# Memory attention and token/channel mixer on one core: an attention schedule with shifted due times

## The chip, the cores and the metric

The kernel runs on one core of a Trainium2 chip. The metric is device time in microseconds (us) of one execution, from the launch to the end. The core's engines are TensorE (PE in the profile, with PEld for its weight loads), VectorE (DVE), ScalarE (ACT), GpSimd (POOL) and SyncE (SP, which issues DMAs only). Each engine takes its instructions in the order in which the program recorded them, and waits for the others by semaphores.

## The reference

Eight batches of eight heads, 576 tokens, head size 64, 32 memory slots. The attention first pools keys and values into the slots and then lets the queries attend to them. A mixer follows: over tokens (576 to 256 to 576) and over channels (512 to 1536 to 512), both with a residual.

```python
a = softmax(phi, axis=2)                    # over the tokens' 32 memory scores
k_m = einsum('bhsm,bhsd->bhmd', a, k)
v_m = einsum('bhsm,bhsd->bhmd', a, v)
attn = softmax(q @ k_m.T / sqrt(64), axis=-1)
x = attn @ v_m                              # to (batch, 576, 512)
h = relu(x.T @ w_tok1) @ w_tok2
u = x + h.T
out = u + relu(u @ w_ch1) @ w_ch2
```

## The kernel before

**The products.** Full float32 precision is had from float32r matmuls: each operand is kept as a high part (a rounded copy, made by ScalarE) and a low part (the rest, a subtraction by VectorE, or by GpSimd at a few places), and each product is three matmuls: high by high, high by low, low by high. Nearly all operands therefore pass through ScalarE, then VectorE, before TensorE can use them.

**The work.** The channel mixer runs over nine chunks of 512 tokens. Chunks 0 to 2 are done plainly (line 161 the first product `cp`, 126 and 129 the parts `hh` and `hl` of its relu, 184 the second product into `acc`). From chunk 3 on the first product is built from seven smaller products of quarters, in the tiles `qa` and `qb` (line 322); ScalarE copies them to `whole` (1917), VectorE adds there (1920), and lines 126 and 129 split the relu into `qhh` (or `qal`'s high tile) and `qhl` (or `qal`). The second product (184) of the pair before is mixed in between.

**The attention beside it.** A quad `(b, Q)` is four heads of batch `b`. Its work is one long chain through all engines. `phi` is loaded (line 407), reduced over tokens by VectorE (421, `pr`) and across partitions by GpSimd (432, `prr`), subtracted (435), raised (ACT, 445), and summed (421 and 454). `step_kv` (467) pools keys and values. `scales`, `turn_keys`, `spread_v` (458 to 516) scale them; the keys go through memory and back (519, 528) to become `kb`. `step_s` (566) makes the scores `sp` in two PSUM banks, VectorE turns them (573), and the softmax follows (580 to 597). VectorE turns the result into `aT` (603); `a_pair` makes its high part on ScalarE (638) and its low part (639) on `low_eng`: GpSimd, but VectorE in quads (2,0) and (4,0). `v_pair` (652) then writes `vv` on ScalarE, in the room of `aT`, so it has to wait for the low parts. The softmax also goes to memory as `rows` (663) and comes back as `raw` (670, 673); `nat_full` and `nat_tail` split it (122, 123); `step_A` (708) and `step_R` (727) are the token mixer's first product, each split again (`Ah`, `Al`; `Rh`, `Rl`); `step_u` (748), four times, gives the chunk's input `u`.

**What sets the order.** Attention and mixer share each engine's queue by a table of due times. A unit is one product of the mixer (a chunk has 24), a step is entered with `at(h, fn, k=...)`, and the loop over the mixer calls what is due at its point of the program, in the order of `h`, then `k` (-1, 0, 1), then entry. In chunks 1 and 2, what is due at an even `h` with `k=0` stands ahead of the twelve matmuls of the second product there, and with `k=1` behind them. For each quad, `m` is the unit of `step_kv` and `r` an offset for the scores; `JOINT = (4, 1)` marks the last quad that has its `step_kv` alone. From (5,0) on `step_kv` rides along with the `step_s` of the quad before. `w` shifts the steps of `phi`. The table of quads is `starts` (line 1779): (3,0) has m=38, r=44; (3,1) 49, 54; (4,0) 59, 63.5; (4,1) 69, 74; then (5,0) 79, 86; (5,1) 91, 98; (6,0) 103, 110 and so on in steps of 12.

Chunk 3 begins at unit 72. PSUM has two banks for all attention tiles (tag `at`), so each of them waits for the one before the last to be read. `phi` has two buffers.

Of the kernel before, what the change touches and what calls it, by code (L numbers as in the profile page):

```python
# [28 lines left out]
def kernel(  # L29
# [36 lines left out]
    NF = 2 * w_ch2.shape[0]  # L66
# [1660 lines left out]
    for Q, h0 in ((0, 3), (1, 11)):  # L1727
        qd = quads[1, Q]
        late = 4 if not Q else 0
# [27 lines left out]
    for z in order:  # L1757
        if z.eng == "PE":
# [3 lines left out]
            if gap > 0.3 and z.take:  # L1762

                late = any(y.eng == "SP" and y.ready > z.begin - 0.5 for y in z.after)
# [10 lines left out]
    def at(h, fn, *x, k=0):  # L1775
        events.setdefault((max(h, 0), k), []).append((fn, x))

    JOINT = (4, 1)
    starts = [(2, 0, 24, 24), (2, 1, 34, 34), (3, 0, 38, 44), (3, 1, 49, 54), (4, 0, 59, 63.5), (4, 1, 69, 74)]
    while starts[-1][:2] != (B - 1, 1):  # L1780
        b, Q, m, r = starts[-1]
        starts.append((b + Q, 1 - Q, r + 5, r + NF))
    for b, Q, m, r in starts:
        qd = second if b == 2 and not Q else Quad(b, Q)
        fine = b > 2
        if (b, Q) == (4, 0):
            qd.low_eng = nc.vector
        if qd is not second:
            at(max(m - 11, 2 * NF), qd.load_phi)
            if fine:  # L1790
                w = 1.5 * ((b, Q) == (5, 0))
                at(m - (6 if (b, Q) == (3, 0) else 8.5 - w), qd.phi_max, k=1)
                w -= 1.5 * (JOINT < (b, Q))
                at(m - 4.5 + w, qd.phi_sub)
                at(m - 4 + w, qd.phi_only_exp)
                w += 1.5 * (JOINT < (b, Q))
                at(m - 3.5 + w, qd.phi_sum)
            else:
                at(m - 7, qd.phi_max, k=1)
                at(m - 3, qd.phi_exp, k=1)  # L1800
                at(m - 2, qd.phi_sum, k=1)
            at(loaded + (5 if (b, Q) > (3, 1) else 1), qd.load_kv, k=1)
            at(r - (3 if fine else 4), qd.load_q, k=1)
        joint = JOINT < (b, Q)
        if joint:
            former.follow, loaded = qd, m - 3
        else:
            at(m, qd.step_kv)
            loaded = m
        qd.follow, former = None, qd  # L1810
        at(r + 2, qd.step_s)
        if fine:
            for x, fn in (
                (m + 0.5, qd.scales), (m + 1, qd.turn_keys), (m + 1.5, qd.spread_v),
                (m + 3.5, qd.get_keys), (m + 5, qd.v_high), (m + 6, qd.v_low),
                (r + 2.5, qd.S_max), (r + 3, qd.sub_exp), (r + 4, qd.S_sum), (r + 4.5, qd.S_mul),
                (r + 4.5, qd.rows_out), (r + 5, qd.turn_pairs), (r + 8, qd.nat_full),
                (r + 8.5, qd.nat_tail), (r + 9.5, qd.step_A), (r + 10.5, qd.step_R),
            ):
                at(x, fn)  # L1820
            at(r + 6, qd.rows_in, "qT", 1)
            for x in range(2):
                at(r + 6 + x / 2, qd.a_pair, x)
                at(r + 7 + x / 2, qd.v_pair, x)
            for x in range(4):
                at(r + 12 + x // 2 * 1.5 + x % 2 / 2, qd.step_u, x // 2, x % 2)
            continue
        at(m + 4, qd.values)
        at(m + 1, qd.step_T)
        at(r + 3, qd.sm2)  # L1830
        at(r + (3 if qd is second else 4), qd.a_pair, 1)
        at(r + 6, qd.nat, k=1)
        at(r + 7, qd.v_pairs)
        at(r + 8, qd.step_A)
        at(r + 9, qd.step_R)
        for x in range(4):
            at(r + 10 + x // 2 * (1 if qd is second else 2), qd.step_u, x // 2, x % 2)
    for c in range(2, CHUNKS):
        h = 2 * NF * (c - 1)
        at(h + (9 if c == 2 else 7 if c <= WIN else 1), lambda c=c: mixer(c).take(), k=1)  # L1840
        if c < WIN:
# [3 lines left out]
        late = (  # L1845
            (-6.5, -3, -2.5, -6.5, -3, -2.5, -3.5, -1, -0.5, -1, -0.5, 0, 0.5)
            if c > WIN
            else (-3.5, -3, -2.5, -3.5, -2, -3, -3, -2, -2.5, 0.5, 0.5, 1, 1)
        )
# [217 lines left out]
```

## Time and profile before

| | |
|---|---|
| Median of 3 runs | 769.16 us (767.67 to 769.16) |
| The profiled execution, in all | 765.83 us |
| Its span, first to last instruction | 764.0 us |
| Granted TensorE clock | 1.000 |
| PE busy | 750.1 us (98%) |
| PEld busy | 651.4 us (85%) |
| DVE busy | 466.3 us (61%) |
| ACT busy | 337.9 us (44%) |
| POOL busy | 106.6 us (14%) |
| DMA, mean over the span | 193 GB/s |

In the rows of the trace a time is the start in us from the span's start, then the duration, engine, line, operation, and what it writes and reads; in square brackets stands the idle time of the engine ahead of it and what ended that. The list of waits gives, for an instruction and what it waited for, the sum in us, how often, and the longest. SPq and ACTq are the parts of SyncE and ScalarE that issue DMAs.

### The profile page before, as it was taken

To read this page: it belongs to the slowest core of one execution; us is meant where nothing else is said; L and a number is where in the kernel's file an instruction comes from. 1 tells how busy PE (TensorE), PEld (TensorE's weight loads), DVE (VectorE), ACT (ScalarE), POOL (GpSimd) and SP (SyncE) were. 2 spreads that over 40 slices of the span, in tenths; PEclk is the share of its full clock that TensorE was granted. 3 is DMA by queue.
4 is the path that set the end of the run, shared out by engine and by line. 5 is a ranking of instruction groups with operands and counts; after the bars stand their busy time and mean duration, and the time that the engine had idled before them with its cause. 6 is when DMAs were issued, how large, how long until landed. Compare 5 with 4: busy or idle time off the path is not lost.

```text
span 764.0 us, 13356 instructions
## 1 busy us (share of the span) xinstructions
PE 750.1 (98%) x5159; PEld 651.4 (85%) x5159; DVE 466.3 (61%) x878; ACT 337.9 (44%) x771; POOL 106.6 (14%) x92
## 2 busy tenths in 40 slices
PE   9999999999999999999999999999999999999998
PEld 8777788777878878889888988888989999998997
DVE  4989874786567656665766558564855255335234
ACT  5897553242315333453443535353635343333331
POOL 2144343002112132020101101010101000000000
PEclk9999999999999999999999999999999999999999
DMA  9945630684825454867576849584757367556661
GB/s 366 414 176 171 226 104 1 152 262 141 272 48 176 145 175 124 290 183 249 155 257 202 287 132 280 182 270 147 200 190 207 113 190 232 169 165 221 193 184 65
DMA packets 90447, 147.35 MB, mean 193 GB/s; under 512 B 41488, under 2 KB 60304, under 8 KB 86160
## 3 DMA queue, kind: packets, MB, share of 16 engines
q1 hardware_dynamic: 69216, 79.77, 31.5%
q10 hardware_dynamic: 21168, 66.73, 28.1%
q8 instruction: 41, 0.67, 0.3%
q14 instruction: 22, 0.18, 0.1%
HBM read 121.57 MB, written 24.90 MB: 192 GB/s over the span
## 4 chain that ended last, share of the span: by engine, by line
PE 60%; DMA 6%; DVE 5%; SPq 2%; ACT 1%; issue 1%; POOL 0%; ACTq 0%; DVEq 0%; POOLq 0%
PE acc L184 26%; PE qa L322 12%; PE qb L322 9%; PE u L748 5%; PE cp L161 3%; DMA phi<-in_phi_dram 3%; SPq L519 1%; PE Ap L708 1%; DMA rows<-S 1%; PE sp L566 1%; PE sp L467 1%; DMA sums<-c1h 1%; DMA sums<-sums 1%; DVE pr L421 1%; PE Rp L727 1%
## 5 line engine op out<-in xcount | busy, mean ns | idle before, releaser
L184 PE MATMUL acc<-qhh,c 128*128 128x512 f32 x376 | 145.6, 394 | 0.0
L322 PEld LDWEIGHTS qa<-xT,unit 128*128 128x128 f32 x648 | 91.7, 188 | 10.9 <-ACT whole L1917 1.7
L322 PEld LDWEIGHTS qb<-x,unit 128*128 128x128 f32 x648 | 91.7, 188 | 10.2 <-ACT whole L1917 0.8
L1920 DVE TENSOR_TENSOR whole<-whole 128x256 f32<-128x256 f32 x72 | 33.9, 471 | 106.1 <-ACT whole L1917 105.8
L184 PE MATMUL acc<-hh,c 128*128 128x512 f32 x288 | 96.5, 394 | 0.0
L322 PE MATMUL qa<-xT,unit 128*128 128x256 f32 x648 | 94.5, 281 | 0.9 <-ACT whole L1917 0.9
L322 PE MATMUL qb<-x,unit 128*128 128x256 f32 x648 | 94.4, 281 | 0.4 <-ACT whole L1917 0.4
L184 PEld LDWEIGHTS acc<-qhh,c 128*128 128x128 f32 x376 | 70.8, 188 | 11.7 <-issue 3.3
L1917 ACT COPY whole<-qa 128x256 f32<-128x256 f32 x108 | 40.2, 372 | 88.5 <-PE qa L322 86.6
L184 PE MATMUL acc<-qhl,c 128*128 128x512 f32 x188 | 75.1, 400 | 3.4 <-DVE qhl L129 3.4
L184 PE MATMUL acc<-qal,c 128*128 128x512 f32 x276 | 78.2, 394 | 0.0
L184 PEld LDWEIGHTS acc<-hh,c 128*128 128x128 f32 x288 | 54.1, 188 | 13.9 <-issue 2.9
L184 PE MATMUL acc<-hl,c 128*128 128x512 f32 x144 | 56.2, 390 | 0.0
L1917 ACT COPY whole<-qb 128x256 f32<-128x256 f32 x72 | 26.7, 371 | 62.6 <-PE qb L322 62.6
L639 POOL TENSOR_TENSOR a<-aT,a 64x576 fp32r<-64x576 f32 x20 | 30.8, 1542 | 156.7 <-ACT a L638 136.6
L161 PE MATMUL cp<-uh,c1h 128*128 128x512 f32 x144 | 51.4, 397 | 0.0
L161 PE MATMUL cp<-ul,c1h 128*128 128x512 f32 x144 | 50.3, 390 | 0.0
L161 PE MATMUL cp<-uh,c1l 128*128 128x512 f32 x144 | 50.3, 390 | 0.0
L184 PEld LDWEIGHTS acc<-qal,c 128*128 128x128 f32 x276 | 46.2, 189 | 4.2
L129 DVE SCALAR_TENSOR_TENSOR hl<-cp,hh 128x512 fp32r<-128x512 f32 x36 | 24.7, 686 | 36.3 <-ACT hh L126 36.2
L129 DVE SCALAR_TENSOR_TENSOR qhl<-whole,qhh 128x256 fp32r<-128x256 f32 x72 | 32.3, 449 | 21.4 <-ACT qhh L126 21.2
L126 ACT ACTIVATE qhh<-whole 128x256 fp32r<-128x256 f32 x72 | 30.2, 420 | 26.4 <-DVE whole L1920 16.6
(239 smaller groups left out, 1448.2 us busy)
## 6 DMA issues: line engine op xcount, KB each, us to landing
unit<-sums ACTq DMA_DIRECT2D x108, 512.0 KB, 3.9
kv<-in_kv_dram SPq DMA_DIRECT2D x12, 1280.0 KB, 8.0
rawc<-in_w_ch_dram SPq DMA_DIRECT2D x12, 1024.0 KB, 9.4
q<-in_q_dram SPq DMA_DIRECT2D x16, 576.0 KB, 7.1
unit<-sums ACTq DMA_DIRECT2D x36, 256.0 KB, 3.5
sums<-sums SPq DMA_DIRECT2D x12, 512.0 KB, 6.1
phi<-in_phi_dram SPq DMA_DIRECT2D x16, 320.0 KB, 4.2
out_dram<-u SPq DMA_DIRECT2D x5, 1024.0 KB, 4.2
```

Source lines behind the costliest of these rows:

```text
L126: nc.scalar.activation(out=h, in_=ps, func=AF.Relu)
L129: nc.vector.scalar_tensor_tensor(out=l, in0=ps, scalar=0.0, in1=f32(h), op0=ALU.max, op1=ALU.subtract)
L161: nc.tensor.matmul(ps, l[:, a, w], r[:, a], start=n == 0, stop=n == len(mm) - 1)
L184: nc.tensor.matmul(ps, l_[f // 2][:, f % 2, a * P : (a + 1) * P], r[:, w], start=f == start and x == 0, stop=f == end - 1 and x == 2,)
L322: nc.tensor.matmul(ps[:, :HW], l, r, start=first and n == 0, stop=n == len(mm) - 1, skip_group_check=not first,)
L421: nc.vector.tensor_reduce(out=m.rearrange("p (i m) -> p i m", i=4), in_=s.pt.rearrange("p i j m -> p i m j"), axis=AX.X, op=op,)
L467: nc.tensor.matmul(s.kvp[32 * i : 32 * i + 32, : 2 * D], s.pt[:, i, j, :], s.kv[:, :, j, i, :], start=j == 0, stop=j == NC - 1,)
L519: nc.sync.dma_start(out=s.keys[:, i * M : (i + 1) * M].rearrange("(j c) n -> c j n", c=32), in_=T[32 * i : 32 * i + 32, 1].rearrange("p (j ...
L639: s.low_eng.tensor_tensor(out=l, in0=s.aT[own], in1=f32(h), op=ALU.subtract)
L748: nc.tensor.matmul(ps[:, :HALF], a, r, start=x == 0, stop=x == len(mm) - 1)
L1917: nc.scalar.copy(out=to, in_=ps[:, :HW])
L1920: nc.vector.tensor_tensor(out=to, in0=x, in1=y, op=ALU.add)
```

## The change

Six edits to the table, all in attention:

1. `low_eng` becomes VectorE for all quads of batch 4 and later, which is new for (4,1) and (5,0) to (7,1): seven quads, two low parts each.
2. `load_phi` of the quads from (5,0) on stands at `m - 13`, where it was at `m - 11`.
3. In (3,0) `phi_sub`, `phi_only_exp` and `phi_sum` come one unit later.
4. In (3,0) `step_s` stands behind the second product of its unit.
5. In (4,0) `nat_full`, `nat_tail`, `step_A` and `step_R` come half a unit later.
6. In (3,1) the first `step_u` stands behind the second product of its unit.

```diff
-        if (b, Q) == (4, 0):
+        if b > 3:
             qd.low_eng = nc.vector
         if qd is not second:
-            at(max(m - 11, 2 * NF), qd.load_phi)
+            at(max(m - (13 if JOINT < (b, Q) else 11), 2 * NF), qd.load_phi)
             if fine:
                 w = 1.5 * ((b, Q) == (5, 0))
                 at(m - (6 if (b, Q) == (3, 0) else 8.5 - w), qd.phi_max, k=1)
+                w += (b, Q) == (3, 0)
                 w -= 1.5 * (JOINT < (b, Q))
                 at(m - 4.5 + w, qd.phi_sub)
...
-        at(r + 2, qd.step_s)
+        at(r + 2, qd.step_s, k=int((b, Q) == (3, 0)))
         if fine:
+            late = 0.5 * ((b, Q) == (4, 0))
...
-                (r + 4.5, qd.rows_out), (r + 5, qd.turn_pairs), (r + 8, qd.nat_full),
-                (r + 8.5, qd.nat_tail), (r + 9.5, qd.step_A), (r + 10.5, qd.step_R),
+                (r + 4.5, qd.rows_out), (r + 5, qd.turn_pairs), (r + 8 + late, qd.nat_full),
+                (r + 8.5 + late, qd.nat_tail), (r + 9.5 + late, qd.step_A),
+                (r + 10.5 + late, qd.step_R),
...
-                at(r + 12 + x // 2 * 1.5 + x % 2 / 2, qd.step_u, x // 2, x % 2)
+                k = int((b, Q, x) == (3, 1, 0))
+                at(r + 12 + x // 2 * 1.5 + x % 2 / 2, qd.step_u, x // 2, x % 2, k=k)
```

What it moves on the engines is shown at three places. The first is SyncE's queue around the `phi` of quad (6,0), before; `kb`, `q` and `rows` there belong to (5,0), `keys` to (5,1), and `kv` to (6,0):

```order
L417 DMA q_0_3552<-in_q_dram 128x1152
L663 DMA rows_0_3860<-S_0_3784 32x18x32 x4
L670 DMA raw_0_3912<-rows_0_3860 128x4x128
L673 DMA raw_0_3912<-rows_0_3860 64x128
L519 DMA keys_1_3920<-T_1_3917 32x2x32 x4
L407 DMA phi_0_3925<-in_phi_dram 128x640
L412 DMA kv_0_3961<-in_kv_dram 128x2560
```

The same stretch of SyncE's queue in the changed kernel:

```order
L417 DMA q_0_3552<-in_q_dram 128x1152
L407 DMA phi_0_3847<-in_phi_dram 128x640
L663 DMA rows_0_3862<-S_0_3784 32x18x32 x4
L670 DMA raw_0_3914<-rows_0_3862 128x4x128
L673 DMA raw_0_3914<-rows_0_3862 64x128
L519 DMA keys_1_3922<-T_1_3919 32x2x32 x4
L412 DMA kv_0_3961<-in_kv_dram 128x2560
```

The load of `phi` has moved ahead of the writes of `rows`, the two reads of `raw` and the four writes of `keys`, each of which waits for VectorE or for an earlier transfer.

The second is VectorE's queue in the changed kernel, where the low parts of quad (5,0) now stand (tile `a_5_0`, line 639; before, the two rows are missing here and stand on GpSimd, and the rest of the order is the same; line 1924 is the 1920 of before):

```order
L481 TENSOR_SCALAR ms_1_3889<-mask,ps_1_3890 128x6
L639 TENSOR_TENSOR a_5_0_3884<-aT_0_3882,a_5_0_3884 64x576
L515 TENSOR_SCALAR T_1_3919<-sp_5_0_3755,ps_1_3890 128x64
L516 STREAM_TRANSPOSE T_1_3919<-T_1_3919 128x64
L1924 TENSOR_TENSOR whole<-whole 128x256
L639 TENSOR_TENSOR a_5_0_3885<-aT_0_3882,a_5_0_3885 64x576
L496 TENSOR_TENSOR vb_1_3941<-sp_5_0_3755,ms_1_3889 128x256
L276 TENSOR_TENSOR x_4_3828<-u_3127,x_4_3828 128x512
```

One low part stands ahead of the keys of (5,1), and one between the mixer's add (1924) and the values of (5,1).

The third is VectorE's queue at the start of chunk 3, from the first split of a relu to `Rl` of quad (4,0), before:

```order
L129 SCALAR_TENSOR_TENSOR qhl_3_3070<-whole,qhh_3_3069 128x256
L123 TENSOR_TENSOR Al_0_3141<-Ap_0_3125,Ah_0_3140 128x256
L276 TENSOR_TENSOR x_3_3106<-u_2485,x_3_3106 128x512
L276 TENSOR_TENSOR xT_3_3108<-t_3_2666,xT_3_3108 128x512
L237 COPY u_3146<-rest 128x4x256
L202 TENSOR_TENSOR o_2809<-acc_2_2330,o_2809 128x512
L202 TENSOR_TENSOR o_2809<-acc_2_2334,o_2809 128x512
L1920 TENSOR_TENSOR whole<-whole 128x256
L129 SCALAR_TENSOR_TENSOR Rl_0_3181<-Rp_0_3173,Rh_0_3180 128x512
```

And in the changed kernel:

```order
L129 SCALAR_TENSOR_TENSOR qhl_3_3067<-whole,qhh_3_3066 128x256
L276 TENSOR_TENSOR x_3_3106<-u_2485,x_3_3106 128x512
L276 TENSOR_TENSOR xT_3_3108<-t_3_2666,xT_3_3108 128x512
L237 COPY u_3127<-rest 128x4x256
L202 TENSOR_TENSOR o_2809<-acc_2_2330,o_2809 128x512
L123 TENSOR_TENSOR Al_0_3156<-Ap_0_3140,Ah_0_3155 128x256
L202 TENSOR_TENSOR o_2809<-acc_2_2334,o_2809 128x512
L1924 TENSOR_TENSOR whole<-whole 128x256
L1924 TENSOR_TENSOR whole<-qb_3_3092,whole 128x256
L129 SCALAR_TENSOR_TENSOR qhl_3_3069<-whole,qhh_3_3068 128x256
L129 SCALAR_TENSOR_TENSOR Rl_0_3194<-Rp_0_3186,Rh_0_3193 128x512
```

`Al` has moved behind four instructions that stood behind it, and `Rl` behind one more add and one more split.

## The prediction

> **What bounds the kernel now.** I read the page's head first, then the list of waits by engine, then the timeline at each place where the change moves something. The head of the page gives busy time, share of the span and instructions of each engine:
>
> ```profile
> span 764.0 us, 13356 instructions
> ...
> PE 750.1 (98%) x5159; PEld 651.4 (85%) x5159; DVE 466.3 (61%) x878; ACT 337.9 (44%) x771; POOL 106.6 (14%) x92
> ```
>
> TensorE is the bound: it is idle for 764.0 - 750.1 = 13.9 us only. The change leaves TensorE's work as it is, so it can gain only out of these 13.9 us, and lose by making new gaps. The list of waits says whose they are; of TensorE's rows I show those that the change can reach:
>
> ```profile
> PE acc L184 <- DVE qhl L129: 3.4, 4, 1.3
> ...
> PE kvp L467 <- DVE ul L216: 1.0, 1, 1.0
> PE qa L322 <- ACT whole L1917: 0.9, 1, 0.9
> PE u L748 <- DVE S L573: 0.7, 1, 0.7
> ...
> PE qb L322 <- ACT whole L1917: 0.4, 1, 0.4
> PE sp L566 <- DVE ul L216: 0.2, 1, 0.2
> ```
>
> They are 3.4 + 1.0 + 0.9 + 0.7 + 0.4 + 0.2 = 6.6 us, each at a place where the table of due times sets what stands ahead of what. VectorE's list names the first one's cause, and the only price that the trace has for a low part waiting on VectorE:
>
> ```profile
> DVE pr L421 <- DMA phi<-in_phi_dram: 8.5, 5, 2.4
> ...
> DVE a L639 <- ACT a L638: 1.4, 2, 0.7
> ```
>
> **Edit 2: `phi` two units earlier.** The chain through quad (6,0), on SyncE, VectorE, ScalarE and TensorE in turn:
>
> ```profile
> 374.33 2.50 SPq L663 DMA_DIRECT2D rows<-S  x4
> ...
> 382.34 0.43 SPq L407 DMA_DIRECT2D phi<-in_phi_dram  x1
> ```
>
> ```profile
> 384.98 0.29 DVE L123 TENSOR_TENSOR nat<-raw,nat 64x128 fp32r<-64x128 f32 x1
> 387.63 1.27 DVE L421 TENSOR_REDUCE pr<-phi 128x128 f32<-128x640 f32 x1 [2.36 <-DMA phi<-in_phi_dram]
> 388.81 0.42 DVE L129 SCALAR_TENSOR_TENSOR qhl<-whole,qhh 128x256 fp32r<-128x256 f32 x1
> ```
>
> ```profile
> 386.25 0.42 ACT L126 ACTIVATE qhh<-whole 128x256 fp32r<-128x256 f32 x1 [2.19 <-DMA unit<-sums]
> ```
>
> ```profile
> 387.55 0.39 PE L184 MATMUL acc<-qhh,c 128*128 128x512 f32 x1
> 389.29 0.50 PE L184 MATMUL acc<-qhl,c 128*128 128x512 f32 x1 [1.35 <-DVE qhl L129]
> ```
>
> `phi` is issued at 382.34 and VectorE gets it at 387.63, 5.3 us later. VectorE was free at 384.98 + 0.29 = 385.27 and stood still for 2.36 us, and behind `phi_max` stood the mixer's `qhl`, for which TensorE waited 1.35 us. In the new order the load stands ahead of `rows`, which is issued at 374.33, so it lands by 374.33 + 5.3 = 379.6 at the latest, long before 385.27. `phi_max` then runs from 385.27 to 386.54. Next late is ScalarE's `qhh`, done at 386.25 + 0.42 = 386.67; `qhl` follows at about 387.1. TensorE wants it at 389.29 - 1.35 = 387.94, so 0.8 us of cover is left and the wait goes whole.
>
> Four waits of 3.4 us in all hang on this. The matmul behind such a wait also takes 0.50 us where its neighbour takes 0.39, so I add 0.1 for each. The term is 3.4 + 0.4 = 3.8 us, bounded by 3.0 (one of the smaller waits stays) and 4.3 (0.2 for each restart). The load now passes four writes of `rows`, two reads of `raw` and four writes of `keys`, and delays them by its own 0.43 us of issue at a time when SyncE mostly waits for `S` and `T`: nothing.
>
> **Edit 1: low parts on VectorE.** All L639 rows of the trace, then VectorE around the two GpSimd pieces of quad (5,0):
>
> ```profile
> L639 POOL TENSOR_TENSOR a<-aT,a x20: 1422/1432/2301, 185.0 to 583.2; 64x576 fp32r<-64x576 f32 x20
> ...
> L639 DVE TENSOR_TENSOR a<-aT,a x4: 752/753/755, 146.7 to 303.4; 64x576 fp32r<-64x576 f32 x4
> ```
>
> ```profile
> 377.40 0.98 DVE L1920 TENSOR_TENSOR whole<-whole 128x256 f32<-128x256 f32 x1
> ...
> 378.64 1.59 DVE L276 TENSOR_TENSOR x<-u,x 128x512 fp32r<-128x512 f32 x1
> ...
> 382.82 0.42 DVE L1920 TENSOR_TENSOR whole<-whole 128x256 f32<-128x256 f32 x1 [0.92 <-ACT whole L1917]
> ...
> 389.48 0.69 DVE L276 TENSOR_TENSOR xT<-t,xT 128x512 fp32r<-128x512 f32 x1
> ```
>
> A pair costs VectorE 2 x 0.753 = 1.51 us. But while GpSimd works on its pair, VectorE's own instructions are stretched: the add takes 0.98 us against 0.42, the subtraction 1.59 against 0.69. That is 0.56 + 0.90 = 1.46 us given back, and 0.92 us of idle time stands behind. So the pair costs the later VectorE work nothing, in the seven quads alike. If the stretch stayed, each quad would owe 1.51 - 0.92 = 0.6 us, most of it in the 0.8 us of cover above. The gain is at one place: in (4,1) ScalarE waits for GpSimd with `vv`, and the mixer's copy stands behind it:
>
> ```profile
> 338.97 0.61 ACT L652 CAST vv<-vh 64x128 fp32r<-64x128 f32 x2 [1.44 <-POOL a L639]
> ...
> 340.13 0.37 ACT L1917 COPY whole<-qb 128x256 f32<-128x256 f32 x1
> ```
>
> This is the `qb` wait of 0.4 us in TensorE's list. VectorE is done with a low part 1.43 - 0.75 = 0.7 us sooner than GpSimd, so the wait should go: 0.4 + 0.1 = 0.5 us, bounds 0 and 0.6.
>
> **Edits 3, 4 and 6: three steps of batch 3.** VectorE ahead of the `kvp` wait, and TensorE at it, at two runs of the scores, and at a second product:
>
> ```profile
> 165.63 0.81 DVE L435 TENSOR_TENSOR phi<-phi,prr 128x640 f32<-128x640 f32 x1
> ...
> 166.97 0.61 DVE L216 TENSOR_TENSOR ul<-u,uh 128x288 fp32r<-128x288 f32 x2
> ```
>
> ```profile
> 167.47 1.30 PE L467 MATMUL kvp<-kv,phi 128*32 128x128 f32 x40 [0.99 <-DVE ul L216]
> ...
> 213.00 0.67 PE L566 MATMUL sp<-q,kb 64*32 64x288 f32 x2
> 213.91 0.71 PE L566 MATMUL sp<-q,kb 64*32 64x288 f32 x14 [0.24 <-DVE ul L216]
> ...
> 283.41 0.71 PE L566 MATMUL sp<-q,kb 64*32 64x288 f32 x16
> ...
> 285.97 0.40 PE L184 MATMUL acc<-hh,c 128*128 128x512 f32 x1
> ...
> 288.49 0.39 PE L184 MATMUL acc<-hh,c 128*128 128x512 f32 x1
> ```
>
> With `phi_sub` (L435) a unit later, its 0.81 us no longer stand ahead of `ul`, and `kvp` starts up to 0.8 earlier of its 0.99: I take 0.7 (0 if something else slips in, 1.0 if all goes). The scores of (3,0) start at 213.00 and end at 214.62, 1.62 us for what takes 0.71 at 283.41; behind the second product both of their banks are free: 0.9 (at least the 0.2 of the list). `step_u` of (3,1) waits 0.7 us for `S`. The twelve matmuls of the second product, from 285.97 to 288.49 + 0.23, are 2.75 us long and now stand in between: 0.7 (0 to 0.8). The steps pushed back are each late by a unit at most, about 3 us, and nobody in TensorE's list waits for them there.
>
> **Edit 5: `nat`, `A` and `R` of (4,0) half a unit later.** ScalarE, VectorE and TensorE at the start of chunk 3:
>
> ```profile
> 307.23 0.62 ACT L122 CAST nat<-raw 128x512 fp32r<-128x512 f32 x1 [1.83 <-DMA raw<-rows]
> ...
> 307.75 0.37 ACT L1917 COPY whole<-qa 128x256 f32<-128x256 f32 x1
> ```
>
> ```profile
> 307.88 1.01 DVE L123 TENSOR_TENSOR nat<-raw,nat 128x512 fp32r<-128x512 f32 x2 [2.24 <-ACT nat L122]
> ...
> 312.04 0.43 DVE L123 TENSOR_TENSOR Al<-Ap,Ah 128x256 fp32r<-128x256 f32 x1
> ...
> 315.71 0.70 DVE L129 SCALAR_TENSOR_TENSOR Rl<-Rp,Rh 128x512 fp32r<-128x512 f32 x1
> ```
>
> ```profile
> 316.46 0.40 PE L748 MATMUL u<-w2h,Rl 128*128 128x288 f32 x1
> ```
>
> The copy of `qa` at 307.75 no longer stands behind `nat`, which waits for a DMA; so the 0.9 us wait of `qa` goes. But VectorE still begins with the same `nat` and has work without a gap from 307.88 to `Rl`. `Rl` now stands behind one more add and one more split, 0.33 us start to start each, so it is done 0.66 later, and its matmul moves from 316.46 to about 317.1 or later. What TensorE saves at 308 it waits for again at `R`, whose third matmul needs the later `Al`, or at `u`, with some more. I take a loss of 0.7 us; bounds are a loss of 1.3 (both low parts late by 0.66) and a gain of 1.4 (the 0.9 stays saved, and the 0.5 us that `Rl` now has as slack comes too, if `raw` lands earlier).
>
> **The sum.** 3.8 + 0.5 + 0.7 + 0.9 + 0.7 - 0.7 = 5.9 us. The profiled execution is 765.83 us, its span 764.0; it becomes 759.9. The median of 769.16 lies 3.3 us above it, and I take the same sum off: 763.3.
>
> **Rivals.**
> (a) Edit 5 has no price: the waits at 308 simply go, and the sum is 5.9 + 0.7 + 1.4 = 8.0, so 761.2. For it: `raw` is the last to arrive there, and earlier terms shift it too. Against it: VectorE has no gap in these 8 us. Chance 0.17.
> (b) The change doesn't do what it says: `phi` lands no earlier, because SyncE or the buffer holds it at the new place too. Then 3.8 goes from the sum, and the time is 769.16 - 2.1 = 767.1. Against it: `rows`, behind which it no longer stands, is issued 8 us before it. Chance 0.05.
> (c) A low part holds VectorE until ScalarE's high part is there, at the 0.7 us of L639 in VectorE's list, in all seven quads: 4.9 us, leaving 1.0, so 768.2. Against it: in the new order the low parts stand behind other work. Chance 0.08. [...]
> (d) The slower side: the same hold, and the stretch of VectorE stays, so that the pair's own 1.51 us is owed too. Per quad 0.7 + 1.51 - 0.92 = 1.29, times seven 9.0, so 5.9 - 9.0 is a loss of 3.1: 772.3. It is slower from the point where a quad sends over (5.9 + 1.5) / 7 = 1.1 us on to TensorE. Against it: the 0.98 and 1.59 are seen only beside GpSimd. Chance 0.06.
>
> **How the numbers follow.** The forecast, 763.3, has the remaining 0.64. With all terms at their low ends the gain is 3.0 + 0 + 0 + 0.2 + 0 - 1.3 = 1.9, with all at their high ends 4.3 + 0.6 + 1.0 + 0.9 + 0.8 + 1.4 = 9.0; so the range is 760.2 to 767.3, which leaves out (c) and (d), 0.14. About 0.2%, 1.5 us, is what a measurement of this kernel can tell from no change: faster by more are the forecast, (a) and (b), 0.86; the same is (c), 0.08; slower is (d), 0.06.
>
> **What would show it.** Right: `pr` no longer waits for `phi` in VectorE's list, `acc` behind `qhl` is gone from TensorE's, the `qb` and `u` rows too, the scores of (3,0) take 0.71, L1920 and L276 keep 0.42 and 0.69 beside the low parts, and TensorE's idle time is about 8 us. A wait of about 0.7 to 1.5 us stands at `R` or `u` of (4,0). Wrong: waits for `a` L638 on VectorE with `qhl` behind, L276 still at 1.6, or a busy PE other than 750.

## The result and the profile after

The changed kernel takes 771.38 us (median of 10 runs, 770.0 to 777.67), the kernel before in the same measurement 766.62 us (10 runs, 763.95 to 769.16). The ratio is 1.0069, with a 95% interval of 1.0042 to 1.0095: slower by 3.2 to 7.3 us, where 5.9 us of gain were forecast. The profiled execution of the changed kernel took 773.63 us, 2.3 above its median. The head of its page:

```profile
span 771.8 us, 13321 instructions
## 1 busy us (share of the span) xinstructions
PE 750.7 (97%) x5159; PEld 652.5 (85%) x5159; DVE 469.4 (61%) x892; ACT 337.3 (44%) x771; POOL 86.0 (11%) x78
```

TensorE is as busy as it was (750.1 before), so the loss is idle time: 771.8 - 750.7 = 21.1 us where there were 13.9. TensorE's rows in the list of waits of the changed kernel:

```profile
PE pp L1085 <- POOL mask L91: 11.0, 1, 11.0
PE sp L467 <- DMA kv<-in_kv_dram: 1.9, 1, 1.9
PE Ap L708 <- DVE nat L123: 1.2, 4, 0.5
PE Rp L727 <- DVE Al L123: 0.9, 1, 0.9
PE qb L322 <- ACT whole L1921: 0.5, 1, 0.5
...
PE kvp L467 <- DVE ul L216: 0.2, 1, 0.2
PE u L748 <- DVE Rl L129: 0.2, 1, 0.2
```

All six waits that the prediction set out to remove are gone or small: `acc` behind `qhl` (3.4 us), `qa` (0.9), `u` behind `S` (0.7) and the scores' 0.2 aren't in the list any more, `kvp` has 0.2 left of 1.0, and the `qb` wait here is another one, at 315.69. But the first row, the wait for GpSimd at the very start, is 11.0 us, where it was 1.6 us before. No edit touches anything there. The second and fourth rows are new, and `Ap` behind VectorE's `nat` has grown from 0.5 to 1.2 us; the new waits and the longest one of `Ap` lie at the start of chunk 3, as does the `qb` wait.

A matmul that both traces have can be compared by its start. This table is worked out from the timelines of TensorE; the fourth column is how late the changed kernel is at that point:

| matmul | before, us | after, us | later by | what happened since the row above |
|---|---|---|---|---|
| first `pp` | 1.57 | 11.00 | 9.43 | GpSimd's start |
| `kvp` of (3,0) | 167.47 | 175.66 | 8.19 | edit 3, and 0.47 of a wait at 81 that no edit touches |
| second `u` tile of (3,1) | 288.72 | 295.26 | 6.54 | edits 4 and 6 |
| `qa` | 308.17 | 313.62 | 5.45 | edit 5: the wait behind `nat` |
| `sp<-kv,phi` | 318.98 | 329.53 | 10.55 | edit 5: all the rest |
| `qb` | 340.55 | 352.01 | 11.46 | matmuls at half clock after the `kv` wait (1.4), edit 1 (-0.5) |
| `acc<-qhl` | 389.29 | 398.46 | 9.17 | edit 2 |
| `acc<-qhl` | 512.71 | 520.64 | 7.93 | edit 2, and 1.0 lost at `Ap` of 436 |

In this execution the granted TensorE clock falls to 0.50 from 331 to 334 us, right behind the `kv` wait; in the kernel before it is 1.00 throughout this stretch.

So the edits 1 to 4 and 6 gave what was forecast, edit 5 cost several times its price, and 9.4 us are lost before any of it begins. GpSimd's first rows, of the kernel before:

```profile
0.72 0.20 POOL masks.py:197 MEMSET ident<- 128x128 f32 x1 [0.29 <-POOLq L2045]
1.22 0.29 POOL masks.py:199 TENSOR_SCALAR_AFFINE_SELECT ident<-ident 128x128 f32<-128x128 f32 x1 [0.30 <-POOL ident masks.py:197]
```

and of the changed kernel:

```profile
0.72 0.20 POOL masks.py:197 MEMSET ident<- 128x128 f32 x1 [0.29 <-POOLq L2049]
10.66 0.28 POOL masks.py:199 TENSOR_SCALAR_AFFINE_SELECT ident<-ident 128x128 f32<-128x128 f32 x1 [9.74 <-issue]
```

The memset runs at the same 0.72 us. Then the select on the identity matrix, the first instruction that isn't a memset, waits 9.74 us for nothing that the profile shows ("issue"). Everything at the start hangs on the identity and the masks behind it. Ahead of the select both traces have the same two instructions of GpSimd's queue (first the kernel before, then the changed kernel; the durations are in ns, the last two times are the starts in us):

```profile
masks.py:199 POOLq MODIFY_POOL_CONFIG  x2: 11/14/16, 1.1 to 1.1; - x2
```

```profile
masks.py:199 POOLq MODIFY_POOL_CONFIG  x2: 11/11/11, 0.9 to 1.0; - x2
```

Before, the select follows them within 0.1 us; in the changed kernel, 9.7 us later.

### The profile page after: what moved, and what is told of

It reads as the page before. It is cut to its first block, busy times and chain, and to the rows that moved or that the text cites. A ratio compares the mean times of both kernels' runs of the same rounds, so it can differ in the third digit from the quotient of the medians.

```text
span 771.8 us, 13321 instructions
## 1 busy us (share of the span) xinstructions
PE 750.7 (97%) x5159; PEld 652.5 (85%) x5159; DVE 469.4 (61%) x892; ACT 337.3 (44%) x771; POOL 86.0 (11%) x78
## 4 chain that ended last, share of the span: by engine, by line
PE 79%; DVE 7%; DMA 5%; issue 5%; ACT 2%; POOL 1%; SPq 1%; ACTq 0%; POOLq 0%; DVEq 0%
PE acc L184 32%; PE qa L322 12%; PE qb L322 9%; PE cp L161 8%; PE u L748 7%; PE Ap L708 3%; DMA raw<-rows 2%; PE u L1406 2%; DMA rows<-S 2%; PE sp L566 1%; DMA kv<-in_kv_dram 1%; PE Rp L727 1%; PE sp L467 1%; DMA sums<-c1h 1%; PE end L184 1%
## 5 line engine op out<-in xcount | busy, mean ns | idle before, releaser
L1924 DVE TENSOR_TENSOR whole<-whole 128x256 f32<-128x256 f32 x72 | 30.4, 422 | 101.9 <-ACT whole L1921 101.7
L184 PEld LDWEIGHTS acc<-hh,c 128*128 128x128 f32 x288 | 54.1, 188 | 13.9 <-issue 2.5
L129 DVE SCALAR_TENSOR_TENSOR qhl<-whole,qhh 128x256 fp32r<-128x256 f32 x72 | 30.4, 422 | 19.2 <-ACT qhh L126 18.4
L184 PEld LDWEIGHTS acc<-qhl,c 128*128 128x128 f32 x188 | 36.1, 192 | 0.7
```

The lines of the kernel that those rows point to most:

```text
L129: nc.vector.scalar_tensor_tensor(out=l, in0=ps, scalar=0.0, in1=f32(h), op0=ALU.max, op1=ALU.subtract)
L184: nc.tensor.matmul(ps, l_[f // 2][:, f % 2, a * P : (a + 1) * P], r[:, w], start=f == start and x == 0, stop=f == end - 1 and x == 2,)
L1924: nc.vector.tensor_tensor(out=to, in0=x, in1=y, op=ALU.add)
```

## Experiments

Two theories on the start. A: the start depends on the state in which the execution before left GpSimd, since going on with another kind of instruction than its last one costs it time. Before, GpSimd's last work was the low parts (a tensor_tensor), and the select started at 1.22 us; with edit 1 it is a partition reduction, and the select starts at 10.66 us. B: the late start belongs to that one execution, or to the size of GpSimd's program. The first five kernels below decide this, the next five are on edit 5, and the last two on the rest of the edits.

The kernel before already has a row that speaks for A. In mid-kernel its GpSimd changes 22 times between tensor_tensors and reductions, and each time it stands idle for 5.79 us or more; most of these times hold a wait for data as well. Two reductions in a row follow each other after 0.19 us at 163.50. At the change with the shortest idle time the profile shows nothing that is waited for:

```profile
207.24 5.04 POOL L196 TENSOR_TENSOR o<-uh,ul 128x512 f32<-128x512 f32 x4 [8.31 <-DMA kb<-keys]
218.07 1.09 POOL L454 PARTITION_ALL_REDUCE psr<-pr  x1 [5.79 <-issue]
```

A pair of MODIFY_POOL_CONFIG stands ahead of each change, here at 212.5 us.

**A tensor_tensor last on GpSimd.** The changed kernel with the line below (`spare` is a tile of its own, 128x1, read by nobody):

```diff
     assert not events, events
+    nc.gpsimd.tensor_tensor(out=spare, in0=two, in1=two, op=ALU.add)
```

> The changed kernel with one GpSimd tensor_tensor on a 128x1 tile recorded as the last GpSimd instruction; its result is used by nobody. [...] With the tensor_tensor last, TensorE's first matmul starts at about 1.6 us, and 771.4 - 9.4 = 762.0 us. Rival B (the late start belongs to that one execution, or to the size of GpSimd's program): the time stays at 771.4, and if the late start is seen in the profile it is there with the added instruction too.

Measured: 762.13 us against 765.87, ratio 0.9955 (0.9933 to 0.9977). Two of GpSimd's rows, the second one its last:

```profile
1.21 0.29 POOL masks.py:199 TENSOR_SCALAR_AFFINE_SELECT ident<-ident 128x128 f32<-128x128 f32 x1 [0.29 <-POOL ident masks.py:197]
...
530.78 0.44 POOL L1977 TENSOR_TENSOR spare<-mask 128x1 f32<-128x1 f32 x1 [7.23 <-issue]
```

One instruction of 0.44 us, near the end of GpSimd's work, brings the select back to 1.21 us. In place of the 9.74 us at the start of the changed kernel GpSimd now waits 7.23 us in mid-kernel, ahead of this instruction, where nobody needs it. Theory A holds in sign and size.

**A partition reduction last, in the kernel before.**

```diff
     assert not events, events
+    nc.gpsimd.partition_all_reduce(spare, two, P, RED.max)
```

> The kernel before with one GpSimd partition reduction of a 128x1 tile as its last GpSimd instruction, its result used by nobody. Theory A: this alone brings the late start of the changed kernel into the kernel before: first matmul at about 11 us, 766.6 + 9.4 = 776.0 us. Rival B: no late start, 766.6 us.

Measured: 776.76 us against 765.87, ratio 1.0139 (1.0111 to 1.0167), 8.5 to 12.8 us. GpSimd's rows:

```profile
10.72 0.28 POOL masks.py:199 TENSOR_SCALAR_AFFINE_SELECT ident<-ident 128x128 f32<-128x128 f32 x1 [9.80 <-issue]
...
603.29 0.79 POOL L1973 PARTITION_ALL_REDUCE spare<-mask  x1 [6.18 <-issue]
```

The kernel before, with none of the edits, gets the same late start.

**Edit 1 alone.** The kernel before with

```diff
-        if (b, Q) == (4, 0):
+        if b > 3:
             qd.low_eng = nc.vector
```

> The kernel before with edit 1 alone (low parts of batches 4 and later on VectorE). Theory A: the last GpSimd instruction is a partition reduction, so the late start comes, +9.4, and the qb wait at 340 goes, -0.5: 766.6 + 8.9 = 775.5 us. Rival B: only the qb wait goes, 766.1 us. The recorded prediction's rival of a low part that holds VectorE would show as waits of acc for qhl in TensorE's list and up to 4.9 us more.

Measured: 775.03 us, ratio 1.0124 (1.0087 to 1.0161). The first matmul starts at 11.45 us. Edit 1 is the one that brings the late start. TensorE waits 2.5 us for `qhl` in this trace, 2 times, less than the 3.4 before, so the recorded prediction's rivals of a low part that holds VectorE did not come about.

**A memset last.** The changed kernel with

```diff
     assert not events, events
+    nc.gpsimd.memset(spare, 0.0)
```

> The changed kernel with a GpSimd memset of a 128x1 tile as its last GpSimd instruction. [...] Rival: any further instruction at the end, or one more in the program, is enough: 762.1 us.

Measured: 772.67 us (2 runs), ratio 1.0078 (1.0048 to 1.0108): as slow as the changed kernel.

```profile
11.04 0.28 POOL masks.py:199 TENSOR_SCALAR_AFFINE_SELECT ident<-ident 128x128 f32<-128x128 f32 x1 [10.12 <-issue]
...
534.10 0.17 POOL L1977 MEMSET spare<- 128x1 f32 x1
```

Theory A has the changed kernel's 771.4 us here if a memset, ahead of which the trace shows no MODIFY_POOL_CONFIG, leaves GpSimd as the reduction left it. The memset follows the reduction without a wait, and the select starts at 11.04 us. So one more instruction at the end is not enough.

**The last quad's low parts left on GpSimd,** and no edit 5. The changed kernel with

```diff
-        if b > 3:
+        if 3 < b and (b, Q) != (B - 1, 1):
             qd.low_eng = nc.vector
...
-            late = 0.5 * ((b, Q) == (4, 0))
+            late = 0
```

> The changed kernel without edit 5, with no instruction added, but with the two low parts of the last quad (7,1) left on GpSimd as before, so that its last work is a tensor_tensor by itself. Theory A: no late start, as with the added one: 758.8 us. If not, the added instruction did something else, and the time is 758.8 + 9.4 = 768.2 us.

Measured: 758.96 us against 766.62, ratio 0.9908 (0.9883 to 0.9934), with the select at 1.22 us. No instruction need be added; it is enough which work comes last. The profiled execution was the slowest of the six (763.97 us), and its `kv` row is used below.

**No edit 5, a tensor_tensor last.**

```diff
-            late = 0.5 * ((b, Q) == (4, 0))
+            late = 0
```

> As the first of these kernels (changed kernel with a tensor_tensor last on GpSimd), but without edit 5: nat, A and R of quad (4,0) stand where they stood before. Theory: edit 5 is what costs 5.4 us between 308 and 332 us (the start of q, kb and kv on SyncE waits for nat's last piece on VectorE, Al comes late for R, and the read of raw shares the DMA engines with a unit); the 1.1 us that qa's wait had cost are part of the 5.4 already, as a gain. So 762.0 - 5.4 = 756.6 us, with no kv wait in TensorE's list. Rival: the phi load or the low parts, not edit 5, make raw and kv late there: about 762, with the kv wait still there.

Measured: 758.75 us against 765.87, ratio 0.9907 (0.9884 to 0.993), 5.4 to 8.9 us faster than the kernel before. Edit 5 thus costs 762.13 - 758.75 = 3.4 us, where 5.4 were expected; that figure came from the one trace of the changed kernel, with a `kv` wait of 1.9 us where the kernel with a tensor_tensor last has 1.4, and with the half clock behind it, which that kernel doesn't have. No `kv` wait is in the trace.

**Edit 5 alone.** The kernel before with the `late` lines of the diff.

> The kernel before with edit 5 alone (nat, A, R of (4,0) half a unit later). From the kernels with and without it so far (762.1 against 758.8): +3.4, so 765.9 + 3.4 = 769.3 us, with waits of R for Al (0.9) and of sp for kv (1.4 to 1.9) in TensorE's list. The recorded forecast: +0.7, 766.6 us, without a kv wait. Rival: the kv wait needs edit 2 as well (phi on SyncE), so about +1.5 to 2, 767.7 us.

Measured: 770.44 us against 765.15, ratio 1.0062 (1.0042 to 1.0082), 3.2 to 6.3 us slower. TensorE's list has, beside the waits of before:

```profile
PE qb L322 <- ACT whole L1919: 1.7, 2, 0.9
...
PE Ap L708 <- DVE nat L123: 1.3, 4, 0.6
PE sp L467 <- DMA kv<-in_kv_dram: 1.2, 1, 1.2
...
PE Rp L727 <- DVE Al L123: 0.9, 1, 0.9
```

The `qb` row has 0.4 us, once, in the kernel before; the second wait is 0.79 us at the start of chunk 3. So edit 5 needs no other edit to cost this. Where it comes from shows on four engines. SyncE and TensorE of the kernel before:

```profile
308.91 0.35 SPq L417 DMA_DIRECT2D q<-in_q_dram  x1
...
310.56 0.58 SPq L412 DMA_DIRECT2D kv<-in_kv_dram  x1
```

```profile
318.98 0.42 PE L467 MATMUL sp<-kv,phi 128*32 128x128 f32 x8
```

SyncE, ScalarE, VectorE and TensorE of the changed kernel:

```profile
318.61 0.35 SPq L417 DMA_DIRECT2D q<-in_q_dram  x1
...
320.34 0.53 SPq L412 DMA_DIRECT2D kv<-in_kv_dram  x1
```

```profile
314.74 0.62 ACT L122 CAST nat<-raw 128x512 fp32r<-128x512 f32 x1 [2.42 <-DMA raw<-rows]
...
315.27 0.36 ACT L1921 COPY whole<-qb 128x256 f32<-128x256 f32 x1
```

```profile
315.39 0.69 DVE L123 TENSOR_TENSOR nat<-raw,nat 128x512 fp32r<-128x512 f32 x1 [3.22 <-ACT nat L122]
316.00 1.34 DVE L421 TENSOR_REDUCE pr<-phi 128x128 f32<-128x640 f32 x1
...
318.30 0.28 DVE L123 TENSOR_TENSOR nat<-raw,nat 64x128 fp32r<-64x128 f32 x1
...
321.97 0.41 DVE L123 TENSOR_TENSOR Al<-Ap,Ah 128x256 fp32r<-128x256 f32 x1
```

```profile
322.43 0.39 PE L727 MATMUL Rp<-vh,Al 128*128 128x256 f32 x1 [0.92 <-DVE Al L123]
...
329.53 0.74 PE L467 MATMUL sp<-kv,phi 128*32 128x128 f32 x18 [1.94 <-DMA kv<-in_kv_dram]
```

`raw` and `q` share one buffer (tag `qT`), so the load of `q` is issued only when VectorE has read the last piece of `raw`. Before, that piece was split right behind the first one (one row "x2" at 307.88, both done by 308.89), and `q` left at 308.91. Now `phi_max`, an eviction and an add stand in between; the piece is split at 318.30, 2.9 us behind the first, and `q` leaves at 318.61. Behind `q` on SyncE stands the load of `kv` for (5,0). Before, its data were there 0.35 us ahead of the matmul that needs them (landed 318.63, used 318.98). That cover is gone. And on ScalarE the copy of `qb` now stands behind `nat`, where the copy of `qa` stood before: the wait for `raw` holds up the next copy instead.

**`kv` ahead of `q` on SyncE.** The changed kernel with a tensor_tensor last and

```diff
-            at(loaded + (5 if (b, Q) > (3, 1) else 1), qd.load_kv, k=1)
+            at(loaded + (5 if (b, Q) > (3, 1) else 1) - 3.5 * ((b, Q) == (5, 0)), qd.load_kv, k=1)
```

> The changed kernel with the tensor_tensor last on GpSimd (762.1 us), and on SyncE the load of kv of quad (5,0) ahead of the load of q of (4,1), whose issue waits for VectorE's last read of raw in nat (q and raw share one buffer). Theory: kv is late only because it is queued behind that issue; its wait of 1.4 us and the slow matmuls behind it go, 762.1 - 1.7 = 760.4 us; the waits for Al and nat stay. Rival: kv is late by the transfer itself (busy DMA engines), and the time stays at 762.1.

Measured: 760.81 us against 765.15, ratio 0.9934 (0.9915 to 0.9953), where the same kernel without this move has 0.9955 (0.9933 to 0.9977). The intervals overlap, so the time gained by the move isn't shown; the cause of the `kv` wait is, by the trace. `kv` was issued at 304.17 and landed at 310.97, and its wait is gone. In TensorE's list stand:

```profile
PE Ap L708 <- ACT nat L122: 1.0, 2, 0.7
PE Rp L727 <- DVE Al L123: 0.9, 1, 0.9
```

The wait for `Al` is the one at the start of chunk 3 and stays as it was. The waits of `Ap` lie elsewhere (the longest, 0.73 us, at 422); at the start of chunk 3 `Ap` and `qb` don't wait here, since `raw` landed within 3.9 us of its issue, not 5.2. It had landed, at 304.02, before `kv` was issued.

So the place behind `q` is what made `kv` late in that kernel. It isn't the only thing that can: in the profiled execution of the kernel with the last quad's low parts on GpSimd, without edit 5, `q` left at 305.75, but `kv` took 10.7 us to land (308.78 to 319.46; 8.1 us in the kernel before):

```profile
319.60 0.66 PE L467 MATMUL sp<-kv,phi 128*32 128x128 f32 x8 [3.75 <-DMA kv<-in_kv_dram]
```

So that load can cost time without edit 5 too. Why it was slow in that execution stays open. The granted clock is 0.50 there from 318 to 324 us (0.995 in the mean of that execution), which makes it longer still.

**`A` and `R` later, `nat` not.** The changed kernel with a tensor_tensor last and

```diff
-                (r + 4.5, qd.rows_out), (r + 5, qd.turn_pairs), (r + 8 + late, qd.nat_full),
-                (r + 8.5 + late, qd.nat_tail), (r + 9.5 + late, qd.step_A),
+                (r + 4.5, qd.rows_out), (r + 5, qd.turn_pairs), (r + 8, qd.nat_full),
+                (r + 8.5, qd.nat_tail), (r + 9.5 + late, qd.step_A),
```

> The changed kernel with the tensor_tensor last on GpSimd, and of edit 5 only step_A and step_R half a unit later; nat_full and nat_tail stand where they stood before. Theory: the later nat costs the kv wait, the late raw and the waits at Ap, the later A and R cost the wait for Al of 0.9 us alone, so 758.8 + 0.9 = 759.7 us. Rival: A and R are what costs, nearly 762.1 us.

Measured: 758.95 us against 765.15, ratio 0.9913 (0.9895 to 0.9931), the same as with no part of edit 5. `R` waits 0.3 us for `Al`, not 0.9; VectorE is further ahead in this trace, both pieces of `nat` run at once, and `phi_max` behind them.

```profile
304.37 1.01 DVE L123 TENSOR_TENSOR nat<-raw,nat 128x512 fp32r<-128x512 f32 x2 [1.30 <-ACT nat L122]
305.41 1.35 DVE L421 TENSOR_REDUCE pr<-phi 128x128 f32<-128x640 f32 x1
```

**`nat` later, `A` and `R` not,** the other half, with a tensor_tensor last too:

```diff
-                (r + 8.5 + late, qd.nat_tail), (r + 9.5 + late, qd.step_A),
-                (r + 10.5 + late, qd.step_R),
+                (r + 8.5 + late, qd.nat_tail), (r + 9.5, qd.step_A),
+                (r + 10.5, qd.step_R),
```

> The changed kernel with the tensor_tensor last on GpSimd, and of edit 5 only nat_full and nat_tail half a unit later, A and R where they stood: the complement of the one with A and R alone (759.0 us). Theory: nat's later place on ScalarE and VectorE is what costs, by the q and kv loads queued behind its last piece and by Ap, which now waits for that piece at its old place: 758.9 + 1.4 (kv) + about 1.5 (Ap) = about 761.8 us. Rival: only both halves of the edit together cost, and the time is 759.

Measured: 764.45 us against 766.62, ratio 0.9976 (0.9955 to 0.9997); on the same chip the kernel without edit 5 had 0.9908 (0.9883 to 0.9934). `nat` makes the loss, 5.2 us by these ratios, more than the 3 us that were expected:

```profile
PE sp L467 <- DMA kv<-in_kv_dram: 3.0, 1, 3.0
PE Ap L708 <- DVE nat L123: 2.0, 5, 1.0
```

The `kv` wait is longer than in the kernels with the whole edit (1.2 to 1.9), and the granted clock falls to about 0.5 behind it, from 322 to 325 us (0.998 in the mean of that execution). Whether half the edit costs more than the whole is not shown: the two intervals overlap (0.9933 to 0.9977 with both halves).

**Edit 2 alone** (`load_phi` at `m - 13` from (5,0) on):

> The kernel before with edit 2 alone (phi of quads from (5,0) on loaded at m - 13). The last GpSimd work is a low part, so no late start. The recorded forecast for this term: the four waits of acc for qhl go, -3.8, 765.9 - 3.8 = 762.1 us. Rival: the load, now ahead of rows and raw on SyncE, makes raw late for nat, seen in the changed kernel as two new waits of 0.7 us in all at Ap at 436 us: 765.9 - 3.8 + 0.7 = 762.8 or more, with new Ap waits for nat in TensorE's list.

Measured: 760.78 us against 765.15, ratio 0.9938 (0.9922 to 0.9954), 3.5 to 6.0 us faster. `acc` behind `qhl` is gone from TensorE's list; the waits at `Ap` for VectorE's `nat` are 0.7 us in all, 0.2 more than before, so the rival's new waits are nearly absent here.

**Edits 3, 4 and 6 alone** (the lines of the diff on (3,0) and (3,1)):

> The kernel before with edits 3, 4 and 6 alone (the three of batch 3). The recorded forecast: 0.7 + 0.9 + 0.7 = 2.3 us, 765.2 - 2.3 = 762.9 us, with the waits of kvp, sp and u gone from TensorE's list. Rival: what is gained there is lost again by the start of chunk 3, where raw is waited for, and the time stays within 1 us of 765.2.

Measured: 763.60 us against 766.62, ratio 0.9968 (0.9948 to 0.9988), 0.9 to 4.0 us faster. `sp` behind `ul` and `u` are gone from TensorE's list, and `kvp` has 0.3 left. Rows that these edits don't aim at moved as well in this one trace (`acc` behind `qhl` from 3.4 to 1.7 us, `qb` from 0.4 to 1.1, a new wait of 0.8 for another `kv`), so the median confirms the sign and the order of the size, and the three places have to be read one by one.

## Why the prediction was wrong

**Edit 2 was right.** 3.8 us were forecast, and 4.4 us of median came out of the edit alone. In the changed kernel the `phi` of (6,0) is issued 37.7 us before its use and reaches VectorE without a wait. It took 9.4 us to land, not the 5.3 of the prediction, which did no harm with so much cover. SyncE, VectorE and TensorE:

```profile
357.96 0.44 SPq L407 DMA_DIRECT2D phi<-in_phi_dram  x1
```

```profile
395.63 1.32 DVE L421 TENSOR_REDUCE pr<-phi 128x128 f32<-128x640 f32 x1
```

```profile
398.46 0.40 PE L184 MATMUL acc<-qhl,c 128*128 128x512 f32 x1
```

`phi_max` starts 0.03 us behind the piece of `nat` in front of it, and `acc<-qhl` has no bracket and takes 0.40 us again. The 1.0 us lost at `Ap` of 436 in the changed kernel comes again in the trace with `kv` ahead (at 422), and not in the one with a tensor_tensor last; what decides it stays open.

**Edits 3, 4 and 6 were right.** 2.3 us were forecast, 3.0 us of median measured (0.9 to 4.0). TensorE in the changed kernel:

```profile
175.66 0.54 PE L467 MATMUL kvp<-kv,phi 128*32 128x128 f32 x12 [0.24 <-DVE ul L216]
...
223.90 0.72 PE L566 MATMUL sp<-q,kb 64*32 64x288 f32 x16
...
294.21 0.29 PE L748 MATMUL u<-a,vv 128*128 128x288 f32 x1
```

`kvp` gained 0.99 - 0.24 = 0.75 us (0.7 forecast), the sixteen matmuls of the scores take 0.72 us again, and `u` doesn't wait.

**Edit 1: what was weighed was right, and the term that decided was not in the sum.** VectorE's work around the low parts of (5,0) in the changed kernel, and its waits for them:

```profile
388.74 0.38 DVE L1924 TENSOR_TENSOR whole<-whole 128x256 f32<-128x256 f32 x1
389.15 0.76 DVE L639 TENSOR_TENSOR a<-aT,a 64x576 fp32r<-64x576 f32 x1
...
390.28 0.68 DVE L276 TENSOR_TENSOR x<-u,x 128x512 fp32r<-128x512 f32 x1
```

```profile
DVE a L639 <- ACT a L638: 3.5, 7, 1.3
```

The stretch is gone as forecast (0.98 to 0.38, 1.59 to 0.68), the `qb` wait at 340 too (also with edit 1 alone), and 3.5 us of waits at low parts never reach TensorE: the rivals (c) and (d) are refuted. The step that failed is "the pair costs the later VectorE work nothing, in the seven quads alike. [...] The gain is at one place". It followed the work to the engine that takes it over, and did not ask what the engine that gives it up does last: GpSimd's side of the move is put at nothing. With the low parts gone, GpSimd's last work is a partition reduction, and its first select in the profiled execution comes 9.4 us later (10.66 us, where it was 1.22). That this is the cause is shown from both sides: the reduction put last slows the kernel before by 10.9 us of median, and the tensor_tensor put last takes 771.4 to 762.1. The medians move, so it isn't a matter of profiled executions alone. The price of such a change, 5.79 us, stood in GpSimd's rows of the kernel before. What GpSimd does in these 9.7 us, behind the two MODIFY_POOL_CONFIG, no row shows. In mid-kernel, GpSimd waited 7.23 and 6.18 us ahead of the added instructions, for nothing that the profile shows either; at the start it is 9.7 to 10.2 us, and why it is more there stays open. That the state outlasts the execution is the reading of these runs: a last instruction moved the first select from 10.66 to 1.21 us, and in the kernel before from 1.22 to 10.72. The record doesn't say which program ran ahead of an execution, and no run tests what a different program in between would do.

**Edit 5: the mechanism was half seen, and mis-sized.** 0.7 us were forecast; alone it costs 3.2 to 6.3. The wait of `R` for `Al` came as described (0.92 us), and the wait of `qa` went. Four things fail in the step "What TensorE saves at 308 it waits for again at `R`, [...] or at `u`, with some more. I take a loss of 0.7 us". It did not see that the copy of `qb` comes to stand behind `nat` in place of the copy of `qa`: TensorE waits there, 0.50 us in the changed kernel and 0.7 to 0.8 in three more with the whole edit. It took VectorE's order as starting "with the same `nat`", but only the first piece stayed there; the second went behind `phi_max`, an eviction and an add. It did not follow that piece to SyncE, where `q` and behind it `kv` are queued for the buffer. And `Ap` waits for the late piece as well (0.54 us at 318.64). The halves of the edit show that `nat` does it, and `A` and `R` alone cost nothing that can be measured. Rival (a), that edit 5 is free, falls too.

**The sum, mended.** The forecast's terms without edit 5 are 5.9 + 0.7 = 6.6 us of gain; the kernel without edit 5 and with a tensor_tensor last measured 0.9907 of 765.87, 7.1 us (5.4 to 8.9). With edit 5, 3.4 us less, and with GpSimd's late start 9.4 less: 6.6 - 3.4 - 9.4 = a loss of 6.2, where 3.2 to 7.3 were measured. Nothing large is left unexplained. The forecast of the time, 763.3, also stood on a base that was too high: the three runs ahead of it had a median of 769.16, the ten of the result 766.62. The profiled execution of the changed kernel lost 5.4 us net at the start of chunk 3, where the medians say 3.4. Some 0.5 us of that are the longer `kv` wait (1.94 against 1.4 with a tensor_tensor last), and 1.4 to 1.5 the half clock: from the matmul behind the `kv` wait to the next `qb` it takes 22.48 us, and 20.97 in the kernel with a memset last, which has the same 1.94 us of `kv` wait and keeps its clock at 1.00. Why the clock fell in one and not in the other stays open. So does why the read of `raw` takes longer with `nat` late: 4.9 to 5.2 us in five kernels (309.65 to 314.72 in the changed one), 3.5 to 4.5 in those without, but 3.9 in the one with `kv` ahead.

The fastest versions are those with all the other edits, without edit 5 or with it for `A` and `R` alone, whose last GpSimd work is a tensor_tensor: 758.75, 758.95 and 758.96 us, 0.7 to 1.2% faster than the kernel before by their intervals.

## What to carry to other kernels

When work leaves an engine, look at what is now the last and the first thing that this engine does: here one instruction at the end of GpSimd's work, at 530.78 us, moved the first select from 10.66 to 1.21 us, and a reader of a single profile sees the cost at the start, hundreds of microseconds from the edit. Follow every moved instruction to the buffers that it frees and to the DMA queue that waits for them, with all that is queued behind; the 0.35 us between the landing of `kv` and its use were no cover here. An edit of six parts is six predictions: edit 2 paid here by itself, and so did edits 3, 4 and 6 together; edit 1 costs 9 us by itself, and 5 costs 3 to 6. No kernel has all but edit 1, so its own gain of 0.5 us is read from the traces alone.

## What the runs showed of the hardware

GpSimd's first select started at 1.21 or 1.22 us when the last GpSimd work of the program was a tensor_tensor, and at 10.66 to 11.11 us when it was a partition reduction, with a memset behind it or not. In mid-kernel, the change from one kind to the other cost GpSimd 6.18 us (to an added reduction) and 7.23 us (to an added tensor_tensor) of waiting that the profile calls "issue"; an added memset needed none (0.17 us, right behind the reduction). Between two reductions 0.19 us were enough at one place. In the kernel before, the shortest idle time at 22 changes of kind is 5.79 us. Ahead of each of these changes the profile has two MODIFY_POOL_CONFIG, and ahead of the added memset none.

The granted TensorE clock fell to about 0.50 for some 3 to 7 us at waits for `kv` of 1.94, 3.0 and 3.75 us (at the last, already during the wait; the means of these three executions are 0.997, 0.998 and 0.995); at waits of 1.94 us in another kernel, of 1.4 and of 1.2 us it stayed at 1.00 (the means are 0.999, 1.000 and 1.000). What decides it, these six don't show: 1.94 us of wait is on both sides.
